# RetNet recurrence and RWKV channel mix on one core: 64-token chunks from block 3 on, 64x64 transposes from block 3, block 0 mixed without a difference, and a new order of all pieces

## The chip, the cores and the metric

The kernel runs on one core of a Trainium2 chip. The metric is the device time in microseconds. Before the change it is 156.23 us, the median of 3 runs (156.03 to 156.25).

## The reference

Two stages follow each other. The first is a recurrence over 768 tokens for 4 batches and 8 heads of 64 channels; the second mixes channels of its output.

```python
# q, k, v: (4, 8, 768, 64); gamma: one decay per head
for t in range(S):
    state = gamma * state + einsum('bhd,bhe->bhde', k[:, :, t], v[:, :, t])
    y[:, :, t] = scale * einsum('bhd,bhde->bhe', q[:, :, t], state)
x = y.transpose(0, 2, 1, 3).reshape(B, S, 512)
x_prev = x shifted by one token (zero ahead of the first)
xk = mu_k * x + (1.0 - mu_k) * x_prev
xr = mu_r * x + (1.0 - mu_r) * x_prev
k = maximum(xk @ w_k, 0.0)          # 512 -> 1024
v = k * k @ w_v                     # 1024 -> 512
out = sigmoid(xr @ w_r) * v         # float32, (4, 768, 512)
```

## The kernel before

The work is cut into 12 blocks of 256 tokens, three for each batch. Each block goes through an attention part and a channel-mix part. Everything is put in order by hand: `ORDER` is a string of words, one for each piece of work, and a loop at the end of the kernel (L745) calls a function for each word in turn. Every engine carries out its own pieces strictly in the order of the string, and waits where a piece needs another engine's result or a buffer that is still in use. A word is `code.block.more~engine@banks`: `~v`, `~a`, `~p`, `~s` are the vector engine (DVE), the scalar engine (ACT), GpSimd (POOL) and SyncE (SP); `@67` are the PSUM banks that the piece writes (there are eight). Where a word names no engine, the function has its own.

The attention part of block n:

- `lq`, `lk`, `lv` load q, k and v. Most go through POOL's queue, where issuing a load takes POOL's time (rows L232, L237). q and k are turned into float16 on the way. `Q16`, `K16` and `V32` are rings of four buffers, so the load of block n waits until block n-4 has been used. The first two loads (heads 0 to 3 of block 0, on SP) stay float32 and are cast by `cq` and `ck`.
- `vs` (L255) scales v by decays; `Tq`, `Tk` transpose q and k on TensorE (PE), L274 or L280; `Eq`, `Ek` (L243) copy them from PSUM on ACT.
- `S` makes scores k times q; `M` multiplies them by the causal mask on DVE (L349 or L356) and writes them as float16.
- `C` makes k times v for each chunk; `U` (L421) adds that to the state carried from the chunk before; `G` (L426) decays the state for the next block.
- `I` and `J` (L443) give what the carried state adds to y; `Y` (L464, L480 or L491) adds the masked scores times v; `D` (L509 or L516) scales y into `xT` on DVE.

There are three ways to cut a block for this. Blocks 0 and 1 have two chunks of 128 tokens, worked on in halves of 64 partitions (L341, L397, L491). Blocks in `WIDE` have two chunks of 128 tokens, all 128 partitions at once (L333, L386, L480). Blocks in `HALF` have four chunks of 64 tokens (L320, L368, L464): one mask instead of two, two instructions for y instead of one, four sums instead of two. Blocks in `WHOLE` are transposed by 16 matmuls of 128x128 for each of q and k (L274), the others by 32 of 64x64 (L280).

The channel mix of block n: `dx` (L531) makes the difference of x and x shifted by a token; `X.n.w.j` (L560) makes mu times that plus the shifted x, for keys (w=0) and the gate (w=1) and each quarter j of the channels; `K.n.g` are keys (L574 for two blocks together, which `GROUPS` lists, L584 for one); `Qa` (L593) applies relu and `Qb` (L601, L605) squares, both on ACT; `R` (L614) is the gate and `s` (L620) its sigmoid on ACT; `V` (L626) are values, two words for each half of 128 tokens; `O` (L632) multiplies both on DVE; `st` stores on SP. The last half of block 11 is stored in two pieces (`Vc`, `Oc`, `sc`: L644, L651, L659). Blocks in `APART` would be mixed without a difference: `t` (L545) makes (1 - mu) times the shifted x on ACT, and `X` adds mu times x to it on DVE (L554).

`wk`, `wr` and `wv` load weights on POOL, `wk` and `wv` in two halves. `z` are matmuls of zeros: `z.12` means three of float32, the remainder of the count by four is done in float16. `gy` makes a table of decays, `mu`, `mt`, `me` load, turn and copy mu.

Of the kernel before, what the change touches and what calls it, by code (L numbers as in the profile page):

```python
# [38 lines left out]
M.4.0~v Y.3 C.4@67 U.4.0 U.4.1 G.4~a K.2.2@1 Qb.1.1 I.4@23 J.3 Qa.2.1 Qa.2.2 Y.4 Qb.2.0 D.3~v
V.0.0.0@6 Tq.6@45 J.4 dx.3~v V.1.1.0@7 D.4~v dx.4~v X.3.0.1 V.0.1.0@0 V.1.0.0@1 X.2.1.2 Qb.2.2  # L40
wv.1~p V.0.0.1 Eq.6~a V.0.1.1 lq.7~p lk.6~p Tk.6@45 Ek.6~a O.0.0 Tq.7@23 Eq.7~a V.1.0.1 S.6@45
lk.5~p Tk.5@6 X.3.0.2 X.3.0.3 X.3.0.0 K.3.3@2 Qb.2.1 K.3.2@3 O.1.0 Ek.5~a O.0.1 X.3.1.1 M.6~v
lv.5~p vs.5~v K.3.5@0 Qa.3.5 Qa.3.3 K.3.4@6 V.1.1.1 Qa.3.2 lv.6~p C.5@01 S.5@45 Qa.3.4 vs.6~v
C.6@23 Qb.3.3 Qb.3.2 O.1.1 M.5~v U.5.0 X.2.1.3 U.5.1 U.6.0~a U.6.1 U.6.2 U.5.2 U.6.3 K.3.0@6
X.2.1.1 Qa.3.0 Qb.3.0 V.2.0.0@7 K.3.6@4 Qa.3.6 K.3.7@6 st.0.1 Qa.3.7 Qb.3.7 I.5@01 I.6@45 V.2.0.1
K.3.1@3 Qa.3.1 Qb.3.1 X.2.1.0 R.2.0@6 lk.8~p Tk.8@23 lv.7~p Y.5 X.3.1.0 vs.7~v X.3.1.3 Y.6 X.3.1.2
s.2.0 R.3.1@6 D.5~v dx.5~v st.1.1 st.0.0 Ek.8~a X.5.0.3 O.2.0 X.5.0.0 V.2.1.0@2 X.5.0.1 R.3.0@3
D.6~v G.6~a Qb.3.4 s.3.0 s.3.1 lv.8~p R.2.1@0 s.2.1 X.5.1.3 X.5.0.2 R.4.0@1 s.4.0 V.2.1.1 lk.7~p
C.7@67 O.2.1 lk.9~p Tk.9@01 Ek.9~a lv.11~s Tk.7@45 Ek.7~a lq.8~p U.7.0 U.7.1 U.7.2 st.2.0 vs.8~v
K.5.1@3 dx.6~v Qa.5.1 K.5.2@2 I.7@45 S.7@01 U.7.3 K.5.0@6 M.7~v lv.9~p Qb.3.6 Qa.5.0 K.5.3@3  # L50
Qa.5.2 Qb.5.0 R.4.1@6 lk.11~p Qb.3.5 vs.9~v V.4.1.0@7 X.5.1.1 C.8@01 Y.7 D.7~v dx.7~v X.6.0.3
X.6.0.0 lq.11~p Qa.5.3 Qb.5.2 Tq.8@23 X.6.0.2 V.4.1.1 s.4.1 V.4.0.0@6 Eq.8~a V.3.1.0@2 Qb.5.3
Qb.5.1 V.4.0.1 X.6.0.1 lq.9~p G.7~a V.3.0.0@3 V.3.1.1 V.3.0.1 U.8.0 K.6.3@4 Qa.6.3 O.4.0 K.6.1@5
Qa.6.1 Qb.6.1 K.6.2@6 Qa.6.2 lq.10~p O.3.1 U.8.1 st.1.0 X.5.1.0 X.5.1.2 lk.10~p U.8.2 I.8@01 O.3.0
st.2.1 Tq.9@23 Eq.9~a O.4.1 Qb.6.3 S.8@45 M.8~v K.6.0@7 K.6.6@6 Qa.6.0 Qb.6.0 Qa.6.6 X.6.1.3
S.9@23 st.3.1 Tq.11@45 Y.8 Eq.11~a X.6.1.2 R.5.1@7 s.5.1 K.6.7@6 Qb.6.2 K.6.4@4 Qa.6.4 M.9~v D.8~v
dx.8~v X.8.0.0 X.8.0.3 X.8.0.1 X.8.1.1 V.5.0.0@5 R.5.0@7 K.6.5@4 s.5.0 X.6.1.1 Tk.10@01 Qa.6.7
lv.10~p vs.10~v X.6.1.0 C.9@23 U.9.0~v Ek.10~a st.3.0 Tq.10@67 V.5.0.1 O.5.0 X.8.0.2 V.5.1.0@0
R.6.1@1 Qa.6.5 U.9.1 U.9.2 U.9.3 Eq.10~a V.5.1.1 st.5.0 O.5.1 s.6.1 Qb.6.4 S.10@45 I.9@67 C.10@23
G.9~a vs.11~v U.10.0 U.10.1 U.10.2 Qb.6.5 M.10~v st.5.1 R.6.0@1 s.6.0 R.7.0@0 s.7.0 K.8.1@1 Qa.8.1  # L60
K.8.2@2 Qa.8.2 C.11@01 I.10@45 U.10.3 Y.9 K.8.0@3 D.9~v Qb.6.7 K.8.3@2 st.4.1 Tk.11@67 G.10~a
U.11.0 U.11.1 Qa.8.0 Ek.11~a U.11.2 Y.10 D.10~v R.7.1@3 s.7.1 dx.9~v dx.10~v X.9.1.1 I.11@01
X.8.1.0 S.11@67 M.11~v X.9.0.0 Qb.8.2 V.7.0.0@4 Qa.8.3 X.9.0.2 X.9.0.1 V.7.1.0@5 V.6.0.0@3 X.9.0.3
Qb.8.1 Qb.6.6 V.6.1.0@2 V.7.1.1 X.8.1.2 V.7.0.1 V.6.0.1 V.6.1.1 K.9.5@6 K.9.7@7 Qb.8.0 st.4.0
Qa.9.5 O.6.0 Y.11 O.7.1 X.8.1.3 R.8.1@6 D.11~v dx.11~v Qa.9.7 Qb.9.7 K.9.3@5 Qb.9.5 X.11.1.3
X.11.0.1 O.6.1 X.9.1.3 V.8.1.0@7 X.9.1.2 V.8.0.0@3 X.11.0.2 st.6.1 K.9.4@0 Qa.9.4 Qb.9.4 K.9.6@1
Qa.9.6 K.9.0@2 X.9.1.0 K.9.2@0 Qa.9.2 Qb.8.3 X.11.0.3 Qb.9.2 X.11.0.0 Qa.9.3 X.11.1.0 K.9.1@1
R.9.1@0 Qa.9.1 Qb.9.1 X.11.1.2 V.8.0.1 K.11.1@5 O.7.0 Qa.11.1 R.8.0@4 V.8.1.1 Qb.9.3 s.8.0
# [10 lines left out]
def kernel(  # L79
# [180 lines left out]
    def turned(n, a, j0):  # L260
        if whole(n):
            return banks("T", n, a, j0).bitcast(F16).rearrange("c (j i p) -> c j i p", j=NJ, i=2)
        pt = banks("T", n, a, j0).bitcast(F16)[:, :, 0 : 2 * NJ * D]
        return pt.rearrange("c u (j i p) -> c u j i p", j=NJ, i=2)

    def trans(a):
        def go(e, n, j0=0, j1=NJ):
            pt = turned(n, a, j0)
            src = (K16 if a else Q16)(n)
            for j in range(j0, j1):  # L270
                for i in range(2):
                    if whole(n):
                        for s, h, jo, hp in heads(j):
                            nc.tensor.transpose(  # L274
                                pt[low(s), j, i, :], src[:, h, i * D : i * D + D], ident
                            )
                        continue
                    for u in range(2):
                        for s, h, jo, hp in heads(j):
                            nc.tensor.transpose(  # L280
                                pt[low(s), u, j, i, :], src[low(u), h, i * D : i * D + D],
                                ident[low(u), low(u)],
                            )

        return go
# [504 lines left out]
```

## Time and profile before

| what | value |
|---|---|
| median of 3 runs | 156.23 us (156.03 to 156.25) |
| span of the profiled execution | 154.9 us, the only time of its own that the page gives |
| granted TensorE clock | 1.000 |
| PE busy | 146.0 us, 94% |
| DVE busy | 126.9 us, 82% |
| ACT busy | 99.4 us, 64% |
| POOL busy | 55.5 us, 36% |
| first keys matmul starts (L584) | 18.42 us |
| first values matmul starts (L626) | 44.41 us |
| last matmul group starts (L644) | 150.25 us |
| DMA, mean over the span | 144 GB/s, 22.31 MB |

The span runs from the first to the last instruction; the median of the runs is 1.33 us more. The page gives busy time for each engine and slices of the span in tenths. A matmul that waits in its pipeline counts as busy, so the starts in the timeline tell more of PE than its share. In the timeline a row has the start in us, the length in us, the engine, the line, the operation with tiles and shapes, the count, and in brackets the idle time before it with what ended it.

### The profile page before, as it was taken

To read this page: it belongs to the slowest core of one execution; us is meant where nothing else is said; L and a number is where in the kernel's file an instruction comes from. 1 tells how busy PE (TensorE), PEld (TensorE's weight loads), DVE (VectorE), ACT (ScalarE), POOL (GpSimd) and SP (SyncE) were. 2 spreads that over 40 slices of the span, in tenths; PEclk is the share of its full clock that TensorE was granted. 3 is DMA by queue.
4 is the path that set the end of the run, shared out by engine and by line. 5 is a ranking of instruction groups with operands and counts; after the bars stand their busy time and mean duration, and the time that the engine had idled before them with its cause. 6 is when DMAs were issued, how large, how long until landed. Compare 5 with 4: busy or idle time off the path is not lost.

```text
span 154.9 us, 5520 instructions
## 1 busy us (share of the span) xinstructions
PE 146.0 (94%) x2423; PEld 83.9 (54%) x2423; DVE 126.9 (82%) x205; ACT 99.4 (64%) x186; POOL 55.5 (36%) x65
## 2 busy tenths in 40 slices
PE   7779799999999999999999999999999999999990
...
DVE  2588999999899999999999999998999998110541
...
DMA  5999999999999999996999510025000023101254
GB/s 144 263 219 194 197 228 171 196 241 218 156 180 212 199 241 258 223 234 181 116 147 204 150 68 4 4 74 203 4 4 0 6 82 136 52 0 72 96 209 169
DMA packets 45768, 22.31 MB, mean 144 GB/s; under 512 B 37416, under 2 KB 41392, under 8 KB 45744
## 3 DMA queue, kind: packets, MB, share of 16 engines
...
q14 instruction: 5, 0.04, 0.1%
...
## 4 chain that ended last, share of the span: by engine, by line
PE 55%; DVE 24%; DMA 12%; issue 4%; POOL 3%; DVEq 0%; POOLq 0%
PE ps L626 19%; DMA v<-in_v_dram 12%; PE ps L614 9%; PE ps L574 9%; PE ps L584 8%; DVE a L356 3%; DVE xk L560 3%; DVE xr L560 3%; DVE vs L255 3%; DVE dx L531 2%; DVE xT L516 2%; DVE tg L421 2%; DVE os L632 2%; PE ps L443 2%; DVE a L349 1%
## 5 line engine op out<-in xcount | busy, mean ns | idle before, releaser
L626 PE MATMUL ps<-wv,k2s 128*128 128x512 f16 x184 | 43.4, 379 | 0.0
L593 ACT ACTIVATE kr<-ps 128x512 f32<-128x512 f32 x48 | 27.8, 596 | 23.1 <-PE ps L574 18.0
L626 PEld LDWEIGHTS <-k2s 128*128 128x128 f16 x184 | 17.4, 98 | 20.0
L632 DVE SCALAR_TENSOR_TENSOR os<-ps,rs 128x512 f32<-128x512 f32 x23 | 15.4, 683 | 14.5 <-ACT rs L620 7.4
L614 PE MATMUL ps<-wr,xr 128*128 128x512 f16 x96 | 24.1, 380 | 0.0
L584 PE MATMUL ps<-xk,wk 128*128 128x256 f16 x192 | 24.0, 273 | 0.0
L232 POOL DMA_DIRECT2D k<-in_k_dram x20 | 17.7, 898 | 15.2 <-PE ps L280 10.5
L574 PE MATMUL ps<-xk,wk 128*128 128x512 f16 x96 | 22.5, 379 | 0.0
L584 PEld LDWEIGHTS <-wk 128*128 128x128 f16 x192 | 18.1, 98 | 4.9 <-DMA wk<-in_moe_w_k_dram 0.6
L620 ACT ACTIVATE rs<-ps 128x512 f32<-128x512 f32 x24 | 13.7, 594 | 9.3 <-PE ps L614 8.9
L560 DVE SCALAR_TENSOR_TENSOR xr<-dx,mu,xT 128x256 f16<-128x256 f32 (+1 forms) x36 | 19.2, 564 | 0.1
L560 DVE SCALAR_TENSOR_TENSOR xk<-dx,mu,xT 128x256 f16<-128x256 f32 (+1 forms) x36 | 18.8, 567 | 0.2
L232 POOL DMA_DIRECT2D v<-in_v_dram x18 | 16.2, 915 | 1.4 <-DMA q<-in_q_dram 0.5
L243 ACT COPY kT<-ps 128x1024 f16<-128x1024 f16 (+1 forms) x13 | 12.2, 947 | 5.2 <-PE ps L280 4.1
L601 ACT ACTIVATE k2s<-kr 128x512 f16<-128x512 f32 x24 | 14.9, 628 | 0.3
L574 PEld LDWEIGHTS <-wk 128*128 128x128 f16 x96 | 9.2, 98 | 10.8
L531 DVE TENSOR_TENSOR dx<-xT 128x1024 f32<-128x1024 f32 x12 | 14.6, 1223 | 0.3
L605 ACT ACTIVATE k2s<-kr 128x512 f16<-128x512 f32 x24 | 14.5, 628 | 0.1
L243 ACT COPY qT<-ps 128x1024 f16<-128x1024 f16 (+1 forms) x13 | 12.3, 949 | 2.4 <-PE ps L274 2.2
L614 PEld LDWEIGHTS <-xr 128*128 128x128 f16 x96 | 8.8, 97 | 9.2 <-DVE xr L560 0.2
L255 DVE TENSOR_TENSOR vs<-v,csm_sb 128x1024 f16<-128x1024 f32 x10 | 12.1, 1216 | 2.0 <-DMA v<-in_v_dram 2.0
L356 DVE TENSOR_TENSOR a<-ps,c_sb 128x1024 f16<-128x1024 f32 (+1 forms) x12 | 12.2, 1040 | 0.5 <-PE ps L333 0.4
...
## 6 DMA issues: line engine op xcount, KB each, us to landing
...
wk<-in_moe_w_k_dram POOLq DMA_DIRECT2D x2, 512.0 KB, 11.0
...
```

What stands on the lines that cost most here:

```text
L232: e.dma_start(out=dst[:, :, i * D : i * D + D], in_=src[:, i * P : i * P + P].rearrange("h p d -> p h d"),)
L243: e.copy(out=out, in_=in_)
L255: e.tensor_tensor(out=VS(n), in0=V32(n).rearrange("p h (i d) -> p i h d", i=2), in1=gks[:, int(half(n) or wide(n)), :, :, None].to_broadca ...
L356: nc.vector.tensor_tensor(out=a_full(n)[:, i, :, j0:j1], in0=pairs(banks("S", n, i, j0))[:, :, j0:j1], in1=(below if wide(n) else causal[: ...
L531: e.tensor_tensor(out=DX(k)[:, :, m * TM + t0 : m * TM + t1], in0=x[:, :, c + t0 : c + t1], in1=x[:, :, c - 1 + t0 : c - 1 + t1], op=ALU.s ...
L560: nc.vector.scalar_tensor_tensor(out=XM[w](k)[:, j, t0:t1], in0=DX(k)[:, j, t0:t1], scalar=mu[:, w * NCO + j : w * NCO + j + 1], in1=x[:, ...
L574: nc.tensor.matmul(banks("K", n, g), lhsT=wk16[:, co, g * P : g * P + P], rhs=XM[0](k)[:, co, :], start=(co == 0), stop=(co == NCO - 1),)
L584: nc.tensor.matmul(pz[:, i, :], lhsT=wk16[:, co, fo * P : fo * P + P], rhs=XM[0](k)[:, co, m * TM + t0 : m * TM + t1], start=(i == 0 and c ...
L593: nc.scalar.activation(out=kr, in_=banks("K", n, g, *u), func=AF.Relu)
L614: nc.tensor.matmul(banks("R", n, tb), lhsT=XM[1](k)[:, co, t : t + P], rhs=wr16[:, co, :], start=(co == 0), stop=(co == NCO - 1),)
L626: nc.tensor.matmul(banks("V", n, tb), lhsT=K2(n)[:, fo, tb * P : tb * P + P], rhs=wv16[:, fo, :], start=(fo == 0), stop=(fo == NFO - 1),)
L632: nc.vector.scalar_tensor_tensor(out=OS(2 * n + tb), in0=banks("V", n, tb), scalar=1.0 / (KSC * KSC), in1=RS(2 * n + tb), op0=ALU.mult, op ...
```

## The change

Blocks 3 and 4 move from two chunks of 128 tokens to four of 64, as blocks 5 to 11 already have. Blocks 3, 4 and 5 are transposed by 64x64 matmuls. Block 0 is mixed without a difference: `dx.0` goes, eight `t` on ACT come. Four pieces change hands: `ck.0` and the first sums `U.0.0`, `U.3.0`, `U.9.0` go from DVE to ACT, `G.0` and `gy.1` from ACT to DVE; the load of v for block 11 goes from SP to POOL. There are 24 zeros instead of 22. The order string is written anew: in it, block 0's second half of heads and halves of scores come in another order, `wk.0` comes after `lk.2` and `vs.1` on POOL, `wr` before `lk.3`, both `wv` before `lv.3`, `vs.3` after the loads of block 4 and ahead of those of block 5, and the zeros are spread otherwise. The two loads on SP stay the first (`EARLY`).

```diff
--- before.py
+++ after.py
@@ -14,64 +14,69 @@
 
 KSC = 64.0
 KUP = 4.0
-HALF = (5, 6, 7, 8, 9, 10, 11)
+HALF = (3, 4, 5, 6, 7, 8, 9, 10, 11)
 EARLY = ((1, 0, 0), (0, 0, 0))
 GROUPS = ((0,), (1,), (2,), (3, 4), (5,), (6, 7), (8,), (9, 10), (11,))
-APART = ()
-WHOLE = (0, 1, 2, 3, 4, 5)
-WIDE = (2, 3, 4)
+APART = (0,)
+WHOLE = (0, 1, 2)
+WIDE = (2,)
 HEADS = ((0, 1), (3, 2), (4, 5), (7, 6))
 ORDER = """
-lq.0.0.2~s gy.0 lv.0~p lk.0.0.2~s ck.0.0.2~v mu lk.0.2.4~p lq.0.2.4~p gy.1~a lv.1~p lk.1~p lq.1~p
-cq.0.0.2~v lq.2~p wk.0~p z.12@6 Tk.0.0.2@0 Tq.0.0.2@1 Ek.0.0.2~a Eq.0.0.2~a mt@2 wk.1~p vs.0~v
-z.2@6 S.0.0.0.2@01 me M.0.0.0.2~v S.0.1.0.2@45 Tk.0.2.4@2 M.0.1.0.2~v Tq.0.2.4@3 lk.2~p C.0@67
-U.0.0~v Ek.0.2.4~a Eq.0.2.4~a z.1@0 S.0.0.2.4@23 M.0.0.2.4~v I.0@45 S.0.1.2.4@01 M.0.1.2.4~v z.1@2
-Y.0 U.0.1 G.0~a vs.1~p Tk.1@7 Ek.1~a D.0~v dx.0~v lv.2~p lq.3~p lk.3~p C.1@01 U.1.0 X.0.0.0
-X.0.0.3 Tq.1@6 Eq.1~a z.4@2 S.1.1@67 lq.4~p X.0.0.2 I.1@45 Tq.2@0 M.1.1~v S.1.0@23 Eq.2~a wr~p
-X.0.0.1 z.1@7 K.0.0@6 M.1.0~v U.1.1 G.1~a lk.4~p Qa.0.0 X.0.1.0 X.0.1.1 Qb.0.0 Y.1 D.1~v dx.1~v
-X.1.0.1 z.1@3 K.0.3@7 X.1.0.2 Qa.0.3 K.0.2@1 X.1.0.0 Qa.0.2 X.1.0.3 Tk.2@6 K.0.1@0 Ek.2~a vs.2~v
-S.2.0@67 S.2.1@45 M.2.0~v Qb.0.3 K.1.1@1 K.1.2@2 Qa.0.1 Qb.0.2 lv.3~p C.2@0 Qa.1.2 Tq.3@3 Eq.3~a
-U.2.0 I.2@67 Tk.3@0 Qa.1.1 K.1.0@2 Tq.4@1 X.1.1.0 Ek.3~a Qa.1.0 M.2.1~v Y.2 lq.5~p Eq.4~a S.3.0@45
-J.2 X.1.1.1 Qb.1.0 Qb.1.2 X.1.1.2 X.1.1.3 S.3.1@23 lv.4~p K.1.3@0 Qa.1.3 Qb.1.3 wv.0~p X.0.1.3
-X.0.1.2 R.0.0@1 D.2~v dx.2~v X.2.0.2 Qb.0.1 s.0.0 X.2.0.0 lq.6~p R.0.1@6 s.0.1 Tk.4@0 X.2.0.3
...
-Qa.11.3 V.11.0.0@1 s.10.0 Qa.11.2 Qb.11.2 R.10.1@2 V.9.1.1 O.9.1 V.10.1.1 s.10.1 O.10.1 st.9.1
-Qb.11.3 V.9.0.1 st.10.1 s.11.1 Vc.11.1.1@2 s.9.0 V.10.0.0@6 O.9.0 R.11.0@0 V.11.0.1 st.8.0 st.9.0
-s.11.0 Oc.11.1.1 sc.11.1.1~a O.11.0 st.11.0 V.10.0.1 O.10.0 st.10.0 Vc.11.1.0@0 Oc.11.1.0
-sc.11.1.0~s
+mu~a gy.0~v gy.1~v lq.0.0.2~s lk.0.0.2~s ck.0.0.2~a cq.0.0.2~v z.12@6 Tq.0.0.2@0 Eq.0.0.2~a z.2@1
+mt@0 lv.0~p lk.0.2.4~p vs.0~v lq.0.2.4~p Tk.0.0.2@1 me~a Ek.0.0.2~a z.2@2 S.0.1.0.2@01 lv.1~p
+M.0.1.0.2~v Tk.0.2.4@2 Ek.0.2.4~a Tq.0.2.4@3 Eq.0.2.4~a z.2@4 S.0.1.2.4@01 M.0.1.2.4~v S.0.0.2.4@23
+M.0.0.2.4~v C.0@45 U.0.0~a z.1@6 I.0@01 S.0.0.0.2@67 lk.1~p Tk.1@4 U.0.1~v M.0.0.0.2~v Y.0 lq.1~p
+lq.2~p Ek.1~a Tq.1@6 Eq.1~a lk.2~p vs.1~p C.1@45 G.0~v D.0~v t.0.0.0~a z.2@2 S.1.1@01 t.0.0.2~a
+U.1.0~v I.1@67 U.1.1~v M.1.1~v Tq.2@5 S.1.0@23 M.1.0~v Tk.2@4 t.0.0.1~a t.0.1.0~a t.0.0.3~a Ek.2~a
+wk.0~p z.2@0 Y.1 X.0.0.1~v X.0.0.0~v X.0.0.3~v Eq.2~a z.1@0 S.2.1@23 X.0.0.2~v S.2.0@45 t.0.1.3~a
+K.0.0@0 t.0.1.1~a G.1~a Qa.0.0~a Qb.0.0~a D.1~v dx.1~v X.1.0.0~v X.1.0.1~v K.0.1@1 Qa.0.1~a
+X.1.0.2~v wk.1~p K.0.3@0 K.0.2@6 lv.2~p Qb.0.1~a X.1.0.3~v K.1.0@1 Qa.1.0~a M.2.0~v Qa.0.2~a
+Qb.0.2~a K.1.1@7 Qa.1.1~a lq.3~p vs.2~v K.1.2@1 C.2@6 M.2.1~v K.1.3@4 U.2.0~v t.0.1.2~a X.0.1.2~v
+wr~p X.0.1.0~v Qa.1.2~a X.0.1.1~v Qb.1.0~a Tq.3@23 I.2@67 Qa.0.3~a X.0.1.3~v X.1.1.2~v lk.3~p
+Qa.1.3~a wv.0~p wv.1~p X.1.1.3~v lv.3~p Y.2 R.0.1@1 s.0.1~a lq.4~p R.0.0@4 s.0.0~a Qb.0.3~a Tk.3@01
+Ek.3~a X.1.1.0~v X.1.1.1~v J.2 D.2~v R.1.0@5 R.1.1@4 dx.2~v X.2.1.2~v X.2.1.0~v X.2.0.0~v lv.4~p
+X.2.1.3~v X.2.0.2~v X.2.1.1~v V.0.0.0@0 Qb.1.1~a V.1.0.0@1 s.1.0~a V.1.1.0@5 lk.4~p Qb.1.3~a
+Qb.1.2~a X.2.0.1~v V.1.1.1 Eq.3~a S.3@23 M.3~v s.1.1~a O.1.1~v V.0.1.0@4 V.0.1.1 O.0.1~v V.0.0.1
+vs.3~p C.3@45 X.2.0.3~v U.3.0~a Tq.4@23 Eq.4~a K.2.0@6 Qa.2.0~a Qb.2.0~a O.0.0~v U.3.1~v U.3.2~v
+U.3.3~v G.3~a vs.4~v V.1.0.1 K.2.2@0 Qa.2.2~a Qb.2.2~a O.1.0~v st.1.0~s I.3@67 C.4@45 U.4.0~v
+Tk.4@23 lv.5~p Ek.4~a K.2.1@1 Qa.2.1~a K.2.3@0 Qa.2.3~a lq.5~p U.4.1~v U.4.2~v I.4@23 U.4.3~v G.4~a
+vs.5~v S.4@45 M.4~v lk.5~p Y.3 D.3~v R.2.0@1 s.2.0~a Qb.2.1~a lq.6~p Y.4 D.4~v Tq.5@45 Eq.5~a
+Qb.2.3~a lk.7~p st.0.1~s dx.3~v dx.4~v X.3.0.2~v R.2.1@1 s.2.1~a Tk.5@67 Ek.5~a V.2.0.0@4 V.2.0.1
+X.3.0.0~v Tq.6@01 Tk.7@67 Ek.7~a Eq.6~a X.3.0.1~v X.3.0.3~v lv.6~p V.2.1.0@5 V.2.1.1 C.5@67 U.5.0~v
+st.0.0~s S.5@23 K.3.5@0 K.3.2@1 Qa.3.5~a O.2.1~v lq.7~p Qa.3.2~a K.3.0@5 Qb.3.2~a Qa.3.0~a Qb.3.0~a
+K.3.6@1 Qa.3.6~a K.3.4@0 Qa.3.4~a U.5.1~v K.3.1@5 M.5~v X.3.1.2~v lk.6~p Qa.3.1~a vs.6~v C.6@23
+U.5.2~v O.2.0~v st.2.0~s X.3.1.1~v I.5@01 U.6.0~a U.6.1~v Qb.3.4~a Tk.6@67 K.3.3@5 X.3.1.0~v Ek.6~a
+lq.8~p lq.10~p U.6.2~v U.6.3~v Qa.3.3~a X.3.1.3~v lv.7~p Qb.3.1~a K.3.7@4 S.6@67 M.6~v Qa.3.7~a Y.5
...
+X.8.0.3~v K.8.2@4 Qa.8.2~a Qb.6.4~a U.10.3~v M.10~v K.8.1@2 Qa.8.1~a vs.11~v I.9@45 st.5.0~s S.9@01
+M.9~v S.11@67 Qb.8.1~a V.7.0.1 M.11~v O.7.0~v K.8.0@2 Qa.8.0~a G.10~a C.11@01 Y.9 D.9~v I.10@67
+K.8.3@2 U.11.0~v U.11.1~v U.11.2~v st.7.0~s Qa.8.3~a V.7.1.0@3 V.7.1.1 Qb.8.0~a V.8.1.0@2 Qb.8.3~a
+X.8.1.0~v I.11@01 dx.9~v Y.10 D.10~v dx.10~v V.8.0.0@4 Qb.8.2~a X.9.0.1~v X.9.0.0~v V.6.1.0@5
+V.6.1.1 X.9.0.3~v X.9.0.2~v V.6.0.0@6 V.6.0.1 Y.11 V.8.0.1 V.8.1.1 K.9.7@7 Qa.9.7~a D.11~v K.9.5@0
+X.8.1.3~v O.6.1~v st.6.1~s Qa.9.5~a Qb.9.5~a K.9.3@7 X.8.1.1~v X.8.1.2~v R.8.0@5 Qb.9.7~a K.9.4@0
+Qa.9.4~a K.9.2@1 Qa.9.2~a Qb.9.2~a K.9.6@0 Qa.9.3~a Qb.9.3~a K.9.1@1 Qa.9.1~a dx.11~v X.11.0.1~v
...
+Qa.11.0~a O.8.0~v X.9.1.3~v R.10.0@3 R.9.0@1 O.8.1~v Qa.9.0~a Qb.9.0~a Qa.11.3~a K.11.2@2 K.11.1@0
+V.9.0.0@7 Qa.11.2~a Qb.11.2~a s.9.0~a R.10.1@2 s.10.1~a V.9.1.0@1 V.9.0.1 st.7.1~s st.8.1~s V.9.1.1
+O.9.0~v V.10.0.0@2 V.10.0.1 X.11.1.0~v Qb.11.3~a R.9.1@7 s.9.1~a V.10.1.0@6 V.10.1.1 st.8.0~s
+O.9.1~v X.11.1.2~v R.11.0@1 Qb.11.0~a R.11.1@7 Qa.11.1~a Qb.11.1~a Vc.11.1.1@0 s.10.0~a O.10.1~v
+st.10.1~s s.11.1~a V.11.0.0@3 V.11.0.1 O.10.0~v st.9.1~s Oc.11.1.1~v sc.11.1.1~a st.10.0~s st.9.0~s
+s.11.0~a O.11.0~v st.11.0~s Vc.11.1.0@0 Oc.11.1.0~v sc.11.1.0~s
...
@@ -206,7 +211,7 @@
         return n in WIDE
 
     def whole(n):
-        return n in WHOLE or n in WIDE
+        return n in WHOLE
 
     def K2(n):
```

51 lines of the change are left out of this document (17 added, 34 removed).

## The prediction

> **What bounds the kernel now.** I read the page's busy rows first, then PE by stages, then PE's starts in order of time, then the chain and POOL's queue. Busy rows and slices of the page:
>
> ```profile
> PE 146.0 (94%) x2423; PEld 83.9 (54%) x2423; DVE 126.9 (82%) x205; ACT 99.4 (64%) x186; POOL 55.5 (36%) x65
> PE   7779799999999999999999999999999999999990
> DVE  2588999999899999999999999998999998110541
> DMA  5999999999999999996999510025000023101254
> ```
>
> PE and DVE are both full from the fifth slice (about 16 us); DVE gets free at slice 34, PE never; the DMA engines are full for the first 18 slices (70 us). By stages (columns: window, its length, busy PE, PEld, DVE, ACT, POOL, clock, DMA share, GB/s):
>
> ```profile
> 18.40:44.40 26.00, 24.81 (x418) 18.07 (x416) 24.65 (x37) 19.95 (x38) 17.40 (x20) 1.00 1.54 200
> 86.00:130.00 44.00, 43.95 (x810) 23.51 (x809) 42.22 (x71) 27.86 (x52) 0.00 (x0) 1.00 0.17 59
> 130.00:151.30 21.30, 21.29 (x123) 11.75 (x121) 6.30 (x11) 12.78 (x24) 0.00 (x0) 1.00 0.22 83
> ```
>
> A busy PE may still be waiting between matmuls, so I price its work from starts in the timeline:
>
> ```profile
> 50.29 0.45 PE L280 MATMUL ps<-c_sb,k 64*64 64x64 f16 x32
> 50.57 0.44 PE L280 MATMUL ps<-c_sb,q 64*64 64x64 f16 x32
> 50.94 1.04 PE L626 MATMUL ps<-wv,k2s 128*128 128x512 f16 x4
> 51.90 0.45 PE L320 MATMUL ps<-qT,kT 64*64 64x64 f16 x32
> 52.28 0.64 PE L274 MATMUL ps<-c_sb,k 128*64 128x128 f16 x16
> 52.85 0.39 PE L574 MATMUL ps<-xk,wk 128*128 128x512 f16 x1
> ```
>
> 32 small matmuls of 64 columns follow each other in 0.27 us (50.29 to 50.57: 8.4 ns each). Where the next piece has another tile shape it is 0.37 (50.57 to 50.94): 0.1 us a change of shape. Four 512-column matmuls take 0.96 with such a change, 0.86 without (4 x 216 ns). L274's sixteen take 0.57, 0.45 without the change.
>
> With such prices (per matmul: 216 ns at 512 columns, 109 at 256, L274 28, L333 26, L480 27, L386 15.5, 64-column forms 8.4, 64x128 forms 13.5; f32 zeros 0.86 us; 0.105 us per change of shape) I add up PE's pieces in the order string: 139.1 us, of which 104.1 keys, gate and values matmuls and 79 changes of shape. The last matmul group ends at 151.3, so PE lags its own work by about 12 us. Lag = start in the trace minus price of all pieces ahead: 7.7 at the first keys matmul (starts 18.42, 10.7 ahead), 9.9 at the first values matmul (44.41, 34.5), 10.3 at K.3.0 (58.48), 11.8 at R.6.0 (103.73), flat to the end. From 18.4 on only 4.1 us are lost.
>
> What made that lag is in the chain (start, length, what): DVE alone, with short issue gaps, from 43.95 to 75.08, and PE alone after that.
>
> ```profile
> 43.95 1.24 DVE xT L516
> ...
> 74.64 0.43 DVE tg L421
> 75.08 0.04 issue
> 75.12 0.29 PE ps L443 x12
> ```
>
> DVE's pieces summed in the order (back-to-back starts: mask 1.13, dx or whole y 1.26, half y pair 1.45, mix 0.40 or 0.66, sum 0.34, result 0.60, value scaling 1.14) stand at 65.2 us when block 5's keys can start, PE's at 62.0: PE has to wait until its lag is 3.2 above DVE's. So the kernel is PE's sum plus a lag that DVE set.
>
> POOL's queue is in order, and its own scaling waits for a load:
>
> ```profile
> 7.50 1.67 POOL L725 DMA_DIRECT2D wk<-in_moe_w_k_dram  x2
> 9.16 1.78 POOL L232 DMA_DIRECT2D k<-in_k_dram  x2
> 11.00 1.94 POOL L255 TENSOR_TENSOR vs<-v,csm_sb 128x1024 f16<-128x1024 f32 x1
> ```
> ```profile
> 36.97 1.90 POOL L255 TENSOR_TENSOR vs<-v,csm_sb 128x1024 f16<-128x1024 f32 x1 [3.63 <-DMA v<-in_v_dram]
> ```
>
> **The change, part by part.**
>
> *PE.* Six transposes (q and k of blocks 3, 4, 5) go from 16 of L274 (0.45) to 32 of L280 (0.27): -1.1. Blocks 3 and 4 as 64-token chunks: L333 -32 (-0.84), L480 -32 (-0.87), L386 -32 (-0.50); L320 +64 and L368 +64 (+0.53 each), L464 with its inter part +0.78, L443 -0.09: -0.5. Zeros 22 to 24: +0.43. Changes of shape in the new order 79 to 73: -0.6. Sum 137.4, which is 1.7 less, all on PE's path.
>
> A floor per start would turn this round: if a 64-column matmul took L274's 28 ns, the some 440 added ones (L280 192, the three others 64 each, inter parts 56) would cost 440 x 19.6 ns = 8.6 us more. Rows L280 and L320 above, 32 in 0.27 us, speak for 8.4 ns with four 64x64 tiles taking turns; I take that. The Trainium skill has such a floor: the page "TensorE: Matmul & The Clock Gate", section "Wait — 56ns, not 53.3ns?", says that matmul starts never come closer than about 25 ns; by it the 440 would cost 7.3 us more, and the rows here do not agree with it.
>
> *DVE.* Masks four to two -2.27; y in two halves +0.38; sums +1.37 (four more), three first sums given to ACT -1.03; dx.0 gone -1.26; one cast to ACT -0.5; gy.1 and G.0 to DVE +1.03. Sum -2.3 (126.2 to 123.9). What counts more is its place: by the same two sums, block 5's keys now need 62.4 of DVE against 63.3 of PE, blocks 8, 9, 11 need 92.4/93.6, 107.3/109.7, 116.1/117.5. DVE is no longer ahead of PE in any of them; at most it is 0.8 behind once (R.0.1).
>
> *ACT.* Eight weighed copies of 128x256. No such row; the 128x128 scale (L711) starts every 0.30 and the 128x512 square every 0.52, so 0.3 to 0.52, I take 0.39: +3.1. Three sums and a cast +1.7, gy.1 and G.0 away -2.2: +2.6 on an engine with 99 of 155 busy. They lie between 15 and 28 us, beside DVE's masks. Without that cover block 0's mix is late by a copy, 0.4.
>
> *Start.* Walked through with the trace's durations: cq ends 6.4 (gy.1 ahead of it, 0.7), four transposes and scores by 12.4, block 0's last mask 13.1, Y.0 13.9, D.0 15.3, masks of block 1 18.3, four mixes 19.9. K.0.0 could start at 20.0 with 13.4 of PE behind it, against 18.42 with 10.7.
>
> *Loads.* wk.0 now stands on POOL behind lk.2 (1.8) and vs.1: vs.1 waits for lv.1 (10.5 at the earliest by its row), then 1.9, so wk.0 is issued at 12.4 instead of 7.50. What must land ahead of it ends at 16.3 by DMA's pace (before, q2 was through at about 14.3; a k load takes 1.8); wk's two halves then share 5.2 us: wk.0 about 20.3, K.0.0 20.3, lag 6.9. Bounds: 19 (alone on the queue) and 23.1 (as long from issue to landing as before, 18.2-7.5). By the same pace (v 2.0, q 1.5, k 1.8, a weight half 2.6 us, landings up to 2.4 late as v3's was): wr 28, k3 30 to 32, wv.0 32 to 34, wv.1 35 to 37, v3 37 to 39, each within 1 us of its need (29.5, 31, 34, 36, 38.4). vs.3 on POOL holds up lv.5, lq.5, lk.5 and five more; lv.5 is issued at about 41.5, lands 5.9 later at the least (its row), and DVE has vs.5 at 46, ahead of M.4, D.3 and D.4. Not shown by the trace of before: 0 to 2.5, I take 0.6, as four of these needs overlap. The v.11 load moves from SP to POOL's end (1.8, idle there); SP's stores lose a 5.3 wait; neither is on the path.
>
> *Middle.* R.0.1 29.5; first values at 34, lag 8 (before 9.9); vs.3 lets C.3 start at 40.3; K.2.0 41.0; then C.4, M.4, D.3, D.4, both dx in a row (DVE 47 to 54) and four mixes: K.3.5 at 56.4 with 47.3 ahead, lag 9.1. With wk.0's 0.3 and the loads' 0.6: 10.0, no lower than before there (10.1 at K.3.3).
>
> *To the end.* Before gained 1.5 of lag from there, mostly while DVE led. Now, bounds 0.3 and 1.5; I take 1.0 because D.8 to D.11 each come 0.2 to 0.9 us before PE has their y. Lag 11.0. PE ends at 137.4 + 11.0 + 0.3 (the last group's own end) = 148.7. The tail is as before: 151.3 to 154.9, 3.6. Span 152.3. The runs' median is 156.23 for a span of 154.9, 1.33 around it: 153.6.
>
> **The rivals.**
> 1. *Forecast*: PE-paced, lag 10.2 to 12 at the end: 152.8 to 154.6. For it: the two sums above. 0.54.
> 2. *Everything lands in time*: lag 9.5: 152.1. Against it: needs and landings lie within 1 us of each other six times. 0.12.
> 3. *Loads eat most of it*: lag 12.9, 155.5, about even with before. 0.13.
> 4. *Slower*: POOL's two scalings hold the loads behind them. wk.0 lands at 23.1 (+2.8 on K.0.0) and lv.5 at 47.5 or later, with DVE's strict queue behind vs.5 (+1.5): 153.6 + 2.8 + 1.5 = 157.9; it decides once they add 2.6 together, 157 when in part. For it: v3's 11.2 us from issue to landing in the chain of before; against it: DMA is as full in both and no load before vs.1 gets later. 0.20.
> 5. *A floor of 28 ns on every small matmul*: +8.6, 162.2. The rows of 8.4 ns speak against it. 0.01.
>
> A measurement of this kernel can tell 0.2% (0.3 us) from no change. Faster: all of 1 and 2, half of 3: 0.73; same 0.05; slower 0.22. The range takes in rival 2 below and the milder part of rival 4 above: 152.0 to 157.0.
>
> **What would show it.** L280 x576, L320 x288, L349 x9, L356 x8; first L584 at 20 to 20.5, first L626 at 34, first L574 near 57.3, last L644 ending at 148.7, the tail 3.6; DVE's share on the chain well below 24%. Wrong if PE waits for wk after 21, if POOL's vs waits past 39 or DVE's vs stands for v, or if the lag at the first L574 is over 11.5.

## The result and the profile after

The changed kernel takes 168.38 us (168.17 to 168.68, 4 runs) against 156.14 of the kernel before on the same chip: 1.0783 times as long, 95% interval 1.0768 to 1.0798. Forecast was 153.6. (Ratios here leave executions out in which the chip was disturbed, so one can lie below the ratio of two medians.) The profiled execution took 168.17 us with a span of 166.1. Lines of the changed kernel stand 5 higher from the order string on: L589, L619, L631 are keys, gate and values, L285 the 64x64 transposes.

The page of the changed kernel, first busy rows and slices (PEld is TensorE's weight loads):

```profile
PE 147.1 (89%) x2651; PEld 83.6 (50%) x2651; DVE 127.2 (77%) x206; ACT 102.7 (62%) x191; POOL 57.4 (35%) x67
PE   7877879999774799999991999999999999999990
DVE  3567889889987397899991886899999999912422
PEclk9999999999999699999997589999999999999998
DMA  5999999999999969999997012003010002130063
```

PE is busy for about the same time as before, but with holes: slices 11 to 14 (42 to 58 us, 4 of 10 in the third of them), and slice 22 with 1 of 10. Behind each of the two deep ones the granted clock falls (6 in slice 14; 7, 5, 8 in slices 22 to 24). DMA is full to slice 21 (87 us), but for one slice, and so it was before, to slice 22 (85 us): the data fills the queues as long in both kernels. What stands in the holes is in the chain of the changed kernel (start, length, what):

```profile
PE 73%; issue 8%; DVE 8%; DMA 5%; ACT 2%; POOL 1%; DVEq 0%; ACTq 0%; SPq 0%; POOLq 0%
```
```profile
46.71 0.25 PE ps L373 x22
47.09 1.12 issue
48.21 0.34 PE ps L285 x18
...
51.35 0.54 PE ps L619 x2
51.89 3.07 issue
54.96 0.61 PE ps L619 x2
...
86.42 0.59 PE ps L285 x58
87.00 3.67 issue
90.68 0.31 PE ps L285 x6
90.99 0.43 PE ps L469 x25
91.63 5.91 PE ps L631 x16
```

PE stops inside a piece: after two of the four matmuls of a gate piece, after 58 of 64 transposes. The 64 transposes are two pieces of 32, q of block 9 and q of block 8. The last 6 belong to the second, whose q is one load, and whose first 26 transposes have read that load and written the same banks, so no load and no other engine can stop the last 6; the profile names none and says issue. The sixteen values matmuls at 91.63 then take 5.91 us instead of 3.46 (16 x 216 ns), at a lower clock. By the windows (window, length, busy PE, PEld, DVE, ACT, POOL, mean clock over the window, DMA share, GB/s):

```profile
55.00:60.00 5.00, 5.00 (x123) 2.57 (x123) 3.38 (x4) 4.02 (x6) 0.00 (x0) 0.66 1.78 160
90.00:95.00 5.00, 4.32 (x63) 2.06 (x63) 3.05 (x4) 2.89 (x6) 0.00 (x0) 0.50 0.09 30
```

The granted clock itself is 0.50 from 55.4 to 58.8 us and from 89.5 to 96.4, and 1.00 between.

What stops PE is the supply of its own instructions. The page has a DMA queue for them:

```profile
q0 software_dynamic: 38864, 14.95, 69.3%
q8 instruction: 20, 0.33, 0.8%
```

20 packets, each of 16,384 bytes in the trace, and PE has 5312 instructions in the trace (a weight load and a matmul each time): one packet for 256 of them. The kernel before has 19 packets and 4853. Numbering PE's instructions by start, from 0, every long stop stands at 193 plus a multiple of 256, and ends 1.3 to 1.6 us after a packet has landed (a stop is counted here from one start to the next; the idle time that the profile gives is 0.2 to 0.4 less):

| PE's instruction | last before | goes on | stop | packet moves | packet starts after PE entered the 256 ahead |
|---|---|---|---|---|---|
| 449 | 15.66 | 16.76 | 1.10 | 14.51 to 15.40 | 3.57 |
| 705 | 21.51 | 22.95 | 1.44 | 20.42 to 21.31 | 3.66 |
| 1473 | 46.90 | 48.21 | 1.31 | 45.75 to 46.68 | 2.65 |
| 1729 | 51.51 | 54.96 | 3.45 | 52.53 to 53.59 | 4.32 |
| 3265 | 86.81 | 90.68 | 3.87 | 88.34 to 89.36 | 4.41 |
| 3777 | 106.75 | 106.75 | 0 | 103.76 to 104.73 | 0.84 |

This reads as if the packet for the next 256 were asked for when PE enters the 256 ahead of them: it waits 2.7 to 4.4 us while the data queues are full (0.8 to 1.0 where they are empty), moves for about 1, and PE goes on 1.3 to 1.6 later. 256 instructions that run faster than 5.1 to 6.7 us beside full queues, or 3.5 to 3.8 beside nearly empty ones (six of the runs below have such stops, 0.5 to 0.8 us long), end in a stop. At the other counts of this trace the packet starts 0.05 to 3.9 us after the crossing, and three times in the kernel before ahead of it, so the asking is inferred from the stops; the trace has only the packet's movement. Of 64-column matmuls, 8.4 ns each, 128 last 1.1 us. The kernel before has the same stops, small: the longest is 0.56 at instruction 449, inside scores of block 1. Its row of the page, and the stop in its timeline:

```profile
q8 instruction: 19, 0.31, 0.9%
```
```profile
16.29 0.30 PE L341 MATMUL ps<-qT,kT 64*64 64x128 f16 x6 [0.34 <-issue]
```

The five stops are 11.2 us. Lag by the prediction's prices shows how they add up (rows: start less price of all ahead): 7.8 at the first keys matmul, 9.1 behind the stop in it, 10.4 at K.2.0, 11.8 behind the stop at 47, 15.1 behind that at 52, 16.5 behind the low clock, 17.6 at K.5.3, 21.5 behind the stop at 87, 24.2 behind the low clock, and within 0.3 of that to the end. Forecast was 11.0: the 13.2 more are the result, with a tail 0.45 longer; most of what is left of the 14.8 us is time outside the span, 2.0 here, which the forecast took as 1.33. One rise is not a stop for instructions: K.2.0's comes from a wait for DVE ahead of it, where C.3 needs banks that the output of block 0 still holds:

```profile
42.98 0.44 PE L373 MATMUL ps<-vs,k 64*64 64x64 f16 x32 [1.11 <-DVE os L637]
```

### The profile page after: what moved, and what is told of

The parts are those of the page before. It is cut to its first block, busy times and chain, and to the rows that moved or that the text cites. A ratio compares the mean times of both kernels' runs of the same rounds, so it can differ in the third digit from the quotient of the medians.

```text
span 166.1 us, 5985 instructions
## 1 busy us (share of the span) xinstructions
PE 147.1 (89%) x2651; PEld 83.6 (50%) x2651; DVE 127.2 (77%) x206; ACT 102.7 (62%) x191; POOL 57.4 (35%) x67
## 3 DMA queue, kind: packets, MB, share of 16 engines
q1 hardware_dynamic: 4512, 6.69, 11.2%
## 4 chain that ended last, share of the span: by engine, by line
PE 73%; issue 8%; DVE 8%; DMA 5%; ACT 2%; POOL 1%; DVEq 0%; ACTq 0%; SPq 0%; POOLq 0%
PE ps L631 20%; PE ps L589 13%; PE ps L579 13%; PE ps L619 11%; PE ps L285 4%; DMA q<-in_q_dram 4%; PE ps L448 2%; PE ps L469 2%; DVE xr L565 2%; PE ps L373 2%; PE ps L325 2%; DVE os L637 2%; ACT qT L248 2%; DMA out_dram<-os 1%; PE ps L279 1%
## 5 line engine op out<-in xcount | busy, mean ns | idle before, releaser
L631 PE MATMUL ps<-wv,k2s 128*128 128x512 f16 x184 | 45.2, 395 | 0.0
L631 PEld LDWEIGHTS <-k2s 128*128 128x128 f16 x184 | 17.9, 101 | 20.9 <-issue 3.0
L619 PE MATMUL ps<-wr,xr 128*128 128x512 f16 x96 | 24.3, 390 | 3.1 <-issue 3.1
L625 ACT ACTIVATE rs<-ps 128x512 f32<-128x512 f32 x24 | 14.2, 596 | 16.9 <-PE ps L619 14.6
L589 PE MATMUL ps<-xk,wk 128*128 128x256 f16 x192 | 23.3, 273 | 1.2 <-issue 1.2
L579 PE MATMUL ps<-xk,wk 128*128 128x512 f16 x96 | 22.5, 379 | 0.0
L589 PEld LDWEIGHTS <-wk 128*128 128x128 f16 x192 | 18.2, 98 | 5.3 <-issue 1.5
L237 POOL DMA_DIRECT2D v<-in_v_dram x20 | 18.1, 918 | 5.6 <-DVE tg L426 2.7
L514 DVE TENSOR_TENSOR xT<-ps,gy_sb 128x512 f32<-128x512 f32 x18 | 12.4, 690 | 7.9 <-issue 3.9
L565 DVE SCALAR_TENSOR_TENSOR xk<-dx,mu,xT 128x256 f16<-128x256 f32 (+1 forms) x32 | 17.2, 581 | 0.2
L619 PEld LDWEIGHTS <-xr 128*128 128x128 f16 x96 | 9.1, 99 | 13.4 <-issue 3.9
L248 ACT COPY kT<-ps 128x1024 f16<-128x1024 f16 (+1 forms) x13 | 12.2, 948 | 5.6 <-PE ps L279 3.3
L426 DVE TENSOR_TENSOR tg<-ps,tg 128x256 f16<-128x256 f32 x26 | 11.0, 422 | 4.4 <-PE ps L373 2.1
L579 PEld LDWEIGHTS <-wk 128*128 128x128 f16 x96 | 9.0, 97 | 10.6 <-issue 0.3
L242 POOL DMA_DIRECT2D q<-in_q_dram x12 | 10.8, 905 | 9.8 <-PE ps L285 9.2
## 6 DMA issues: line engine op xcount, KB each, us to landing
wv<-in_moe_w_v_dram POOLq DMA_DIRECT2D x2, 512.0 KB, 12.4
wr<-in_moe_w_r_dram POOLq DMA_DIRECT2D x1, 512.0 KB, 11.5
```

The lines of the kernel that those rows point to most:

```text
L237: e.dma_start(out=dst[:, :, i * D : i * D + D], in_=src[:, i * P : i * P + P].rearrange("h p d -> p h d"),)
L248: e.copy(out=out, in_=in_)
L565: nc.vector.scalar_tensor_tensor(out=XM[w](k)[:, j, t0:t1], in0=DX(k)[:, j, t0:t1], scalar=mu[:, w * NCO + j : w * NCO + j + 1], in1=x[:, ...
L579: nc.tensor.matmul(banks("K", n, g), lhsT=wk16[:, co, g * P : g * P + P], rhs=XM[0](k)[:, co, :], start=(co == 0), stop=(co == NCO - 1),)
L589: nc.tensor.matmul(pz[:, i, :], lhsT=wk16[:, co, fo * P : fo * P + P], rhs=XM[0](k)[:, co, m * TM + t0 : m * TM + t1], start=(i == 0 and c ...
L619: nc.tensor.matmul(banks("R", n, tb), lhsT=XM[1](k)[:, co, t : t + P], rhs=wr16[:, co, :], start=(co == 0), stop=(co == NCO - 1),)
```

## The experiments

The theory to be tested: TensorE is short of instructions, wherever many cheap ones stand together while data fills the DMA queues. The rivals: a load comes late; or the new order makes PE wait for DVE or ACT.

**Undo the narrow transposes** of blocks 3 to 5: more PE work, fewer instructions.

```diff
-WHOLE = (0, 1, 2)
+WHOLE = (0, 1, 2, 3, 4, 5)
```

> One part undone: blocks 3 to 5 transposed by 16 matmuls of 128x128 each again instead of 32 of 64x64 (192 instructions of TensorE fewer; by the prices of the prediction 1.6 us MORE of PE). Theory (fetch): TensorE's instructions come by the DMA queue named instruction, one 16 KB packet for 256 of them, and after 168.4 us the kernel stops wherever 256 instructions run faster than the next packet arrives; the two long stops (3.07 us ahead of L619 at 54.96, 3.67 us ahead of L285 at 90.68) lie behind stretches full of 64-column transposes. Then this kernel is FASTER than the changed one though it has more PE work: the stop near 87 to 91 is under 1 us, the clock stays at 1.00 behind it, 160 to 163 us. Rival (late data: q, k, v or weights land late) and rival (order: PE waits for pieces of DVE or ACT): fewer, wider transposes change neither, so 168.4 + 1.6 = 170, or 168.4 if the 1.6 fall into a wait; stops at the same pieces as before.

165.08 us (164.65 to 166.58), 3.3 below the changed kernel although PE has 1.6 us more to do by the prices. The profiled execution took 166.58. Of the 3.67 ahead of the last transposes 1.15 is left (under 1 was expected). The size was missed: the stops at 449 and 705 stayed (1.45 and 1.71), and so did the one at 1729, at another piece than before.

```profile
54.05 0.51 PE ps L279 x14
54.56 3.91 issue
58.47 0.32 PE ps L279 x2
```

The direction goes against both rivals (168.4 or 170); of the sum, 160 to 163, the low clock behind this stop (0.50 from 56.7 to 63.6 us) was not in it.

**Shift the count, not the pieces**: 64 instructions of zeros early.

```diff
-Eq.0.2.4~a z.2@4 S.0.1.2.4@01
+Eq.0.2.4~a z.2@4 pd.32@45 S.0.1.2.4@01
+            nc.tensor.matmul(pz[low(a), u, 0:D], lhsT=z16[low(u), 0:D], rhs=z16[low(u), 0:D], ...)
```

> The changed kernel with 32 matmuls of zeros (64x64 by 64 columns, into two banks that are not in use then) put in behind the fourth zeroing of the start: 64 instructions of TensorE more, 0.3 us of work, no data and no wait of any other piece touched. Theory (fetch): the stops stand at counts of instructions (193 + a multiple of 256) and not at pieces, so each comes 64 instructions earlier in the program: the one in K.0.0 leaves it for the pieces ahead, the one at L285 near 87 (58 of its 64 matmuls done) falls at 26 of 64, the one inside S.4 at 51 falls ahead of S.4; their counts stay 449, 705, 1473, 1729, 3265. Sum of the long stops as before (11 us) give or take 2. Rivals (late data, order): the stops stay at the same pieces, so that their counts go up by 64; time 168.4 to 168.7.

Two executions took 162.92 and 168.75 us, so the time decides nothing. The place of the stop does, in the profile of the second:

```profile
89.44 0.34 PE ps L285 x26
89.77 1.98 issue
91.75 0.50 PE ps L285 x38
```

26 of the 64 transposes where it was 58, which is 32 matmuls earlier, as expected to the instruction. The long stops stand at 449, 705, 1729, 1985 and 3265: at the same grid of counts, though 1473 was let off and 1985 was not; together they are 9.8 us (11, give or take 2, was expected). The order of pieces, loads and waits is the same, and both rivals had the stops stay at their pieces: both fall here.

**Empty the queues earlier**: without the loads of k of block 10 and of q, k, v of block 11. These blocks compute on what their buffers held, so this run leaves out part of the result.

```diff
-lk.10~p ... lq.11~p lk.11~p ... lv.11~p
```

> The changed kernel without the last four head loads (k of block 10, q, k and v of block 11; these blocks then compute on what their buffers held), so that the data queues run empty earlier, from about 80 us on. No piece of PE, DVE or ACT is changed. Theory (fetch): a packet of instructions waits behind the data (4.4 us from the crossing to its start at 83.93 to 88.34, 0.8 to 1.0 us at 102.9 and 106.8 where the queues are empty); so the stop near 87 shrinks from 3.87 to under 1 us, the clock keeps 1.00 behind it, and the time is 161 to 164; the stops at 16.8, 23, 48 and 55 stay. Rival (late data): nothing is waited for from these loads near 87, since block 11 is used from 113 us on only; the stop at 87 stays, 168.4, or less only behind 113. Rival (order): 168.4.

164.81 us (164.30 to 165.13). The same 58 and 6 transposes, the same count, and 0.62 between them instead of 3.67:

```profile
87.48 0.59 PE ps L285 x58
88.07 0.62 issue
88.69 0.25 PE ps L285 x6
...
89.35 3.56 PE ps L631 x16
```

The packet came 1.5 us after it was asked for instead of 4.4, and the values behind the stop run at full clock. The other stops stayed (1.40, 1.44, 1.08, 3.17). The time is 0.8 above the upper end expected.

**Make the kernel before short of instructions**: 96 matmuls of zeros at its start, and the same 96 late, where the queues are empty.

```diff
-z.12@6 Tk.0.0.2@0        (early)
+z.12@6 pd.96@67 Tk.0.0.2@0
-V.6.1.1 K.9.5@6          (late)
+V.6.1.1 pd.96@67 K.9.5@6
```

> The kernel BEFORE with 96 matmuls of zeros (64x64 by 64 columns) behind its first zeroing: 192 instructions of TensorE more, 0.8 us of work at a place where PE waits for loads anyway. Theory (fetch): the counts at which packets are needed move by 192 against the pieces, and one packet's 256 instructions then hold only 2.1 us of work by the prices, at about 66 us, where the data queues are full: a stop of 3 to 4.5 us there, with a lower granted clock behind it; 159 to 162 us. Rivals (late data, order): the kernel before has none of the new order and no late load, and the zeros lie in a wait: 156.2, at most 157.0.

161.77 us (160.53 to 162.30), ratio 1.0363 [1.0291, 1.0435]: as expected. The stop stands at instruction 2497, at a place where the kernel before has none:

```profile
68.72 0.28 PE ps L464 x29
69.00 0.10 PE ps L443 x6
69.10 1.87 issue
70.97 0.25 PE ps L443 x4
```

It is half as long as expected; the rest came earlier (a stop of 1.67 at instruction 705; K.0.3 starts at 22.93 us where it was 20.65) and at 97 us (0.83). The late ones:

> The kernel BEFORE with the same 96 matmuls of zeros (192 instructions of TensorE) as in the run with 96 zeros at the start, now behind the values of block 6 (about 128 us), where the data queues are empty and values and keys matmuls of 216 ns stand around them. Theory (fetch): the packets before stay where they were and the next one arrives in time; only the work itself counts: 0.8 us and two changes of shape, 157.0 to 157.4, no stop over 0.5. Rival (the instructions themselves are dear, 5.6 us for 192 as at the start): 161 to 162.

157.59 us (156.90 to 157.98), ratio 1.0081 [1.0049, 1.0114], 1.3 us instead of 5.7 for the same 192 instructions, 0.2 above the range expected, and a little more than the work itself:

```profile
118.65 0.98 PE L711 MATMUL ps<-zero 64*64 64x64 f16 x96
```

So it is not the instructions but where they stand.

**Fill the queues behind the loads of the kernel before**: 14 loads of 512 KB that nothing reads.

```diff
-lv.10~p vs.10~v
+lv.10~p xl.0~p xl.1~p ... xl.13~p vs.10~v
```

> The kernel BEFORE with 14 loads of 512 KB more, issued by POOL behind its last load (from about 81 us on, two in flight at most), into two buffers of v that are not read any more; nothing waits for them, no instruction of TensorE is added or moved. Theory (fetch): the packets of instructions between 85 and 115 us now wait behind data as those of the first 70 us do; the five times 256 instructions that before took 24.2 us from 87.9 to 112.0 (4.3, 6.3, 4.7, 4.9, 4.0 each) take 5 to 6.7 each: 2 to 8 us more, 158 to 164, with stops called issue. Rival (late data): only loads that are waited for can cost; stores come 1 to 3 us later, which the four output buffers take up: 156.2, at most 157.

159.41 us (158.77 to 160.55), ratio 1.0212 [1.0160, 1.0264], as expected (158 to 164). PE's instructions are those of the kernel before; two stops are new, 1.01 at instruction 3265 and 1.90 at 4289, the first again inside a piece:

```profile
92.00 0.45 PE L320 MATMUL ps<-qT,kT 64*64 64x64 f16 x32
92.27 0.20 PE L280 MATMUL ps<-c_sb,q 64*64 64x64 f16 x4
93.29 0.41 PE L280 MATMUL ps<-c_sb,q 64*64 64x64 f16 x28 [0.82 <-issue]
```
```profile
114.98 0.45 PE L320 MATMUL ps<-qT,kT 64*64 64x64 f16 x32 [1.71 <-ACT kr L593]
```

At the second the profile names a row of ACT (L593, at 114.19); but the kernel before starts this piece at 112.07, ahead of the same row (113.17), so it does not need it, and a packet landed at 113.60, 1.4 ahead of PE's going on. Lag rises by 1.0 and 1.9 at the two stops and by no more than 0.3 anywhere else after 81 us. Data that nobody waits for slows PE by 3 us: the plainest of the runs.

**The chunks alone**: the kernel before with blocks 3 and 4 in four chunks; the words Y.3, D.3, Tq.6, Y.4 and D.4 stand a few places later.

```diff
-HALF = (5, 6, 7, 8, 9, 10, 11)
+HALF = (3, 4, 5, 6, 7, 8, 9, 10, 11)
-WIDE = (2, 3, 4)
+WIDE = (2,)
```

> The kernel BEFORE with blocks 3 and 4 in four chunks of 64 tokens, and nothing else: its order (Y.3, D.3, Tq.6, Y.4, D.4 a few words later, since y of such a block comes in one piece), its 128x128 transposes, its loads. PE has some 256 instructions more, one packet, all of them in the first 70 us; by the prices its work is 0.6 us less, DVE's 1.9 less. Theory (fetch): in that stretch a packet takes 5.1 to 6.75 us; one more costs that, less what PE would have waited anyway: 158 to 163, with stops that the profile calls issue. Rival (order; late data): without the new order and its loads there is nothing to wait for: 155 to 156.5.

161.89 us (161.53 to 165.99), ratio 1.0346 [1.0302, 1.0390], as expected (158 to 163). DVE's 1.9 us and PE's 0.6 are saved and not seen; one stop at instruction 1729 and the clock behind it (0.50 from 52.2 to 55.6) cost more. Timeline of PE:

```profile
48.13 0.35 PE L443 MATMUL ps<-qT,tg 64*64 64x64 f16 x16
50.85 5.31 PE L626 MATMUL ps<-wv,k2s 128*128 128x512 f16 x16 [2.37 <-issue]
```

Lag rises from 12.2 to 16.3 over this stop and the values behind it, and by 1.6 from there to the end (2.1 in the kernel before). Ahead of the stop it has already risen, from 9.3 to 12.2 after 40 us, where the kernel before stays between 9.6 and 9.9: PE waits 1.22 at 42.18 for the scaled v, 0.48 at 44.24 for a sum and 0.48 at 47.62 for y, all from DVE. So this run costs 5.4 us by itself, and some 4 of its lag stand at the stop; whether the waits for DVE belong to the chunks or to the shifted words is not shown.

**All but the chunks and transposes**: the changed kernel with the old chunks and transposes (about as many instructions as before). The new order, block 0 without a difference and the pieces that changed hands stay.

```diff
-HALF = (3, 4, 5, 6, 7, 8, 9, 10, 11)
+HALF = (5, 6, 7, 8, 9, 10, 11)
-WHOLE = (0, 1, 2)
-WIDE = (2,)
+WHOLE = (0, 1, 2, 3, 4, 5)
+WIDE = (2, 3, 4)
-S.3@23 M.3~v ... S.4@45 M.4~v ... Y.3 D.3~v R.2.0@1 s.2.0~a ... Y.4 D.4~v ... R.2.1@1 s.2.1~a
+S.3.0@23 S.3.1@67 M.3.0~v M.3.1~v ... S.4.0@45 M.4.0~v ... Y.3 R.2.0@1 s.2.0~a S.4.1@45 M.4.1~v J.3 D.3~v ... R.2.1@0 s.2.1~a Y.4 J.4 D.4~v
```

> The changed kernel with blocks 3 and 4 in two chunks of 128 tokens and blocks 3 to 5 transposed by 128x128 again; the new order, the loads, the mixing of block 0 and the engines of all pieces stay (S.3, S.4, M.3, M.4 and J.3, J.4 placed where the one piece stood or behind the next). PE has some 464 instructions fewer than the changed kernel, as many as the kernel before. Theory (fetch): with the instructions of before the long stops are gone (none over 1.5 us), the clock stays at 1.00; by the prices PE's sum is 139.8, the lag 11 to 12.5: 155.5 to 158.5. Rivals (late data; the order itself, with its loads behind POOL's scalings and its DVE queue): what costs the 12 us is still there: 165 to 170.

163.39 us (161.87 to 166.30), ratio 1.0376 [1.0330, 1.0423]; expected was 155.5 to 158.5. In the profile, of the execution of 166.30, the stop at instruction 1729 is gone, but 1.4 at 449 and 705 and 2.7 at 2753 are there, and the two masks in a row on DVE hold an output for which C.3 waits:

```profile
45.54 0.46 PE L391 MATMUL ps<-vs,k 128*64 128x64 f16 x16 [2.08 <-DVE os L637]
```

That wait is of this run's placing, and was taken out next:

```diff
-M.3.0~v M.3.1~v s.1.1~a O.1.1~v ... O.0.1~v
+M.3.0~v s.1.1~a O.1.1~v ... O.0.1~v M.3.1~v
```

> The new order with the old chunks and transposes once more, with the second mask of block 3 put behind the outputs O.1.1 and O.0.1 on DVE. In the run before it DVE's two masks in a row stood ahead of these outputs, C.3 waited 2.08 us for their bank, and the clock fell to 0.5 for a slice behind that wait. Theory (fetch): that wait was of my placing; without it 2 to 3 us less than the 162 of that run, 159 to 160.5, and what is left above the kernel before are the stops at counts 449 and 705 (1.4 us each) and near 87 us (2.7). Rival (the wait hides another one, a load or ACT, behind it): 161.5 to 162.5.

160.64 us (159.78 to 161.72), ratio 1.0283 [1.0236, 1.0330]; 159 to 160.5 was expected. So the rest of the change, as it could be placed here, is still 4.3 us slower than before. Stops of 1.51 at 449 and 0.72 at 2753 are part of it, and a granted clock of 0.50 from 17.4 to 20.8 us; the first keys matmul starts with a lag of 9.9 (before 7.7). How much of the rest is the order's, how much is block 0's (the next run) and how much is of my placing of R.2.1, J.3 and J.4 (lag 12.4 to 13.3 around them) stays open.

**Block 0 without a difference, alone**, and then with 16 zeros ahead; and the 16 zeros alone.

```diff
-APART = ()
+APART = (0,)
-U.0.0~v ... D.0~v dx.0~v ... U.3.0~v
+U.0.0~a ... D.0~v t.0.0.0~a t.0.0.3~a t.0.0.2~a ... t.0.0.1~a t.0.1.0~a ... t.0.1.1~a ... t.0.1.3~a t.0.1.2~a ... U.3.0~a
```

> One part of the change alone, that adds no instruction of TensorE: the kernel BEFORE with block 0 mixed without a difference (dx.0, 1.22 us of DVE, goes; eight t on ACT come) and the first sums of blocks 0 and 3 on ACT (0.68 of DVE); order, chunks and transposes as before. Theory (the prediction's step on DVE stands; only the instruction supply was left out of it): DVE alone carries the chain of the kernel before from 44 to 75 us, so DVE's 1.9 us less are worth up to that where PE does not stop for instructions: 154.5 to 155.9. Rival (TensorE is held by its instructions in the first 70 us even before, 256 in each 5.4 to 10.6 us, so that DVE's time there is worth nothing): 156.2 to 156.6. Rival (t on ACT comes late for the first mixes): 156.6 to 157.5.

161.20 us (160.12 to 161.72), ratio 1.0294 [1.0243, 1.0346]: none of the three. ACT is not free there. U.0.0 stood ahead of two copies on its queue, and scores waited:

```profile
11.69 0.31 PE L341 MATMUL ps<-qT,kT 64*64 64x128 f16 x8 [1.15 <-ACT qT L243]
...
14.16 1.07 PE L274 MATMUL ps<-c_sb,k 128*64 128x128 f16 x16
```

Sixteen transposes that take 0.64 before take 1.07 behind that wait, at a lower clock; then a gate mix waits 1.62 for its t, and a stop of 1.07 follows at 705. The lag is 12.5 where it was 8.8, at K.1.0 (32.3 us), and rises afterwards as before. The experiment says that this placement is bad, not what a better one is worth.

> The same with 16 matmuls of zeros of 64x64 by 64 columns behind the first zeroing: 32 instructions, 0.13 us where PE waits for loads. It moves the counts at which packets are needed against the pieces; by PE's prices the stops at 16.3 (0.56) and 62 (0.31) of the kernel before get shorter, the others stay under 0.5. Theory (fetch): 0 to 0.8 us below the kernel without these zeros, 154.0 to 155.9. Rivals: the same time as without them, or 0.1 more.

160.92 us (160.56 to 163.04): no difference that these runs can tell (0.3).

> The kernel BEFORE with 16 matmuls of zeros of 64x64 by 64 columns behind its first zeroing (32 instructions, 0.13 us, where PE waits for loads). Theory (fetch): the packets come at other pieces; by PE's prices no packet of the first 90 us is then shorter than before's shortest (3.8 us at 66), the stops of before (0.56 at 16.3, 0.31 at 62) shrink: 155.4 to 156.3, the one variant that could beat the kernel before. Rivals: 156.2 to 156.6.

159.31 us (157.74 to 159.96), ratio 1.0191 [1.0152, 1.0230]; expected was 155.4 to 156.3. The stop at 16.3 did shrink (0.56 to 0.27), but the one at instruction 1985 grew from 0.31 to 1.33, and y of block 0 (32 matmuls at 12.18 us) took 1.05 us where it took 0.64 before, behind a wait of 0.51 instead of 0.24, at a lower clock. This profile is of the shortest of the six executions, 157.74; what the others lost beyond it is not in it. So the prices do not tell such shifts to a microsecond; no variant that I ran beats the kernel before.

## Why the prediction was wrong

- **PE's sum, 137.4.** The counts came as said (L285 x576, L325 x288, L354 x9), and from 98 us to the end the lag is flat, so the prices hold there. The rival of a floor of 28 ns (162.2) was right in its sign and wrong in its mechanism: 32 transposes still take 0.25 to 0.27 us when their instructions are there.
- **The step that failed** is the one from the sum to the time: lag was carried on as something that only loads and DVE raise. A term is missing, the supply of instructions, which the runs show at 5 to 6.7 us for 128 matmuls beside full queues. From instruction 193 to 3265 the changed kernel needs 79.7 us and the kernel before 81.6, some 6.7 for each 256 in both: 459 instructions more are 1.8 packets, or 12 us by that pace. (The kernel before is not held by it throughout, its stops being short; the runs are the evidence, not this sum.) The changed kernel's five stops are 11.2 us, and the low clock behind two of them cost some 4 more. The profile of before had it to be read: the row q8, and a stop called issue inside the scores of block 1. "128 matmuls in how many us, and what do the queues do meanwhile" was not asked.
- **The gain of 64x64 transposes** (-1.1) was a loss of 3.3 in the run that undid it; **the 64-token chunks** (PE -0.5, DVE's masks -2.27) cost 5.4 in the run of them alone, some 4 of it at one stop. Both traded few wide matmuls for many cheap ones, where data fills the queues. The rest of the change cost 4.3 in its run; the three come to 13.0 against 12.2 measured, but they were taken from different sides and need not add up.
- **DVE leaves the chain.** It did: 24% of the chain before, 8% after. It bought nothing, since PE then stood still for its instructions.
- **Start and loads** were near: the first keys matmul waits for no load, v3 landed by 37.8 (37 to 39), POOL's scaling ended at 39.9. It came at 21.28 instead of 20.3, behind the stop of 1.10 at instruction 449; values at 35.2 instead of 34. C.3 came at 43.0 instead of 40.3, by the wait of 1.11 for DVE's output, which the walk through the middle did not have. Rival 4, loads held by POOL, was not the cause of the slower time.
- **Middle and end**: K.2.0 at 43.7 (41.0), the first L579 at 64.3 (57.3), last lag 24.2 (11.0). The sign of being wrong that was named for it, a lag over 11.5 at that first L579, came with 17.
- **ACT** was priced as cover (0.4 if it is gone). The run with block 0 alone shows the cover is thin there, in the order of the kernel before: 1.15 and 1.62 us of waits from small copies and one sum.
- **Tail**: 0.45 longer, since the last quarter's product waits for a store:

```profile
160.52 0.43 DVE L656 SCALAR_TENSOR_TENSOR os<-ps,rs 128x256 f32<-128x256 f32 x1 [1.89 <-DMA out_dram<-os]
161.41 0.60 ACT L625 ACTIVATE rs<-ps 128x512 f32<-128x512 f32 x1 [2.20 <-DVE os L656]
```
